# Two attentions mixed by a gate, on one core: other steps for four loads, for a copy of sums, for the output projections and for one score in eight

## The chip, the cores and the metric

The kernel runs on one core of one Trainium2 chip. The metric is the device time of one execution in microseconds (us). The figure for a kernel is the median of its runs. A difference of about 0.3% (3.1 us) is what a measurement of this kernel can tell from no change.

## The reference

Two attention layers over the same input x (2048 tokens, width 448, 16 heads of 28) are mixed by a gate for each token. Layer A is linear attention on learned features, layer B is full softmax attention:

```python
x = A_x
g = _sigmoid((x * gate_w).sum(-1, keepdims=True))
...
phi_q = jnp.concatenate([_softmax(pq, axis=-1), _softmax(-pq, axis=-1)], axis=-1)
...
num = jnp.einsum("bhqf,bhfd->bhqd", phi_q, kv)
...
scores = jnp.einsum("bhqd,bhkd->bhqk", q, k) * scale
p = _softmax(scores, axis=-1)
o = jnp.einsum("bhqk,bhkd->bhqd", p, v)
...
return g * a + (1 - g) * b
```

The data are float32; the projections and the scores run as matmuls of 128x512 in fp32r.

## The kernel before, in words

The first third of the span makes the projections, layer A and the first row maxima for layer B. What the change touches is the rest: layer B's attention, which the loop at L1110 writes out step by step.

**Steps.** The 16 heads are four groups g of four heads, and the queries four blocks qb of 512. One pair (g, qb) is called gq here, 0 to 15. Each gq has 16 steps, one for each 128 keys kt, so there are 256 steps s. In a step, `scores` (L846) makes four score tiles st of 128 keys x 512 queries, one for each head, each in its own PSUM bank, and ScalarE (ACT) takes their exponential into four tiles p (L868). One step later `values` (L982) multiplies p by the values into pv, one bank that gathers the sums of four heads over the 16 steps. So TensorE (PE) does scores of step s, then values of step s-1.

**Visits.** The exponent needs each query's largest score subtracted. These maxima nm are found ahead of the scores that use them, by 180 visits (`mx_visit`, L306). A visit is four small matmuls pm into four banks (L323). ACT reads one bank with a relu (L327, tile rl), VectorE (DVE) reads two with a plain maximum (L334) and one with a maximum of that bank plus the rl of the visit before (L331). One visit in four has three plain maxima instead, and the next has one more to do.

**Single and double steps.** Up to step 104 the loop takes two steps at a time with one visit, in 52 rounds (eight scores, sixteen value matmuls, one visit). From 105 to 232 it takes one step with one visit, in 128 rounds. After 232 there are no visits, and it takes two steps again.

**Banks.** There are eight PSUM banks: one for pv, and seven that `cycle_banks` (L917) deals out. Scores and visits read and write different ones in turn. Three banks (`late3`) come from scores and visits of earlier rounds; four (`visit`) were the banks of the visit just before. In a single step the scores take the three of late3 and the first of visit, which is the one that ACT's relu of that visit reads. After 232 one bank is set aside for the output projections (`spare`), and six go round. The order in which L911 asks for the banks first decides which place in PSUM, and so which earlier reader, each of them follows.

**Loads.** The stacked keys kst (five buffers, four for each group) and queries qst (two buffers, one for each gq) come from DRAM in four DMAs of 224 KB each (`load_k`, `load_q`, `load_stack`), and the maxima go into a row of qst by four DMAs of 2 KB (`load_nm`, L838). All DMAs are issued by SyncE's queue (SP). The order on PE, DVE, ACT and POOL is the order in which the program is written; the order on SP is made by the framework's scheduler from the same program. SP is strictly in order: a DMA that waits for POOL or DVE holds up all behind it. Each DMA also uses one of eight completion semaphores in turn, and waits until that semaphore's last DMA has landed.

**After the last key of a gq**, `finish` (L1026) copies pv out on DVE (f1, L400, tile oUb), which frees the pv bank; a little later it sends the sums' denominators through DRAM (f2: den, rd, and rs, which holds them spread over all rows), multiplies on POOL (f3, L421) and splits the result in two parts on POOL (f4, L429 and L430), which go to DRAM as od (L1046), or for the last group straight to the projections. POOL also subtracts keys from each other for the visits (kc, L197).

**Projections.** In the last group, when a query block is done, `project` (L994) makes an output tile of 128 tokens by eleven matmuls into the spare bank (pob, L110), and DVE adds it to layer A's part (acc, L1000), which frees that bank. `PROJ` names the step of the first of four tiles of a block; before the change they run at the end of the round in which that step lies.

Of the kernel before, what the change touches and what calls it, by code (L numbers as in the profile page):

```python
# [8 lines left out]
F32 = mybir.dt.float32  # L9
F32R = mybir.dt.float32r  # L10
U32 = mybir.dt.uint32
AF = mybir.ActivationFunctionType
# [5 lines left out]
P = 128  # L18
# [5 lines left out]
NG = 4  # L24
NT = S // P
NQ = S // 512
SCALE = DH ** -0.5
# [3 lines left out]
LOWEST = -3.0e38  # L31
LAST = 232
OUTS = (200, 238, 246, 206)
PROJ = (234, 242, 250)


def f32(ap):
# [4 lines left out]
def gated_mix_kernel(ctx, tc, xT, wqkB, wvB, wvA, wkAT, wqAT, phi, woA, woB,  # L42
# [260 lines left out]
    flats += [(gq, kb, qt, h, 64 * gq + 16 * kb + 4 * qt + h) for gq in range(GM + 1, NG * NQ)  # L303
              for qt in range(4) for kb in range(4) for h in range(4)]

    def mx_visit():  # L306


        take_diffs(2)
        f = mxs["f"]  # L310
        todo = flats[f:f + 4]
        fins = mxs["fin"][:1 if todo and todo[0][1] == 0 else None]
        del mxs["fin"][:len(fins)]
        mxs["f"] = f + len(todo)
        if todo:
            gq, kb, qt, _, col = todo[0]
            g, qb = divmod(gq, NQ)
            if kb == 1 and qt in (0, QM) and gq + 1 < NG * NQ and ("qc", gq + 1) not in mxs:
                mx_query(gq + 1)
            pm = mx_banks(f, kb)  # L320
            for j in sorted(range(4), key=lambda j: j != kb):
                js = slice(32 * j, 32 * j + DH)
                nc.tensor.matmul(pm[j], mxs[("qc", gq)][js, qt * P:(qt + 1) * P],  # L323
                                 mxs[("kc", g, kb)][js, :], start=True, stop=True,
                                 tile_position=(32 * j, 0))
            rl = late_p.tile([P, 512], F32, tag="rl", name=f"rl{f}", bufs=3)
            nc.scalar.activation(rl, pm[kb], AF.Relu if kb < 3 else AF.Copy)  # L327
            for j in sorted({0, 1, 2, 3} - {kb}, key=lambda j: j == kb - 1):
                if j == kb - 1:
                    r = mxs["rl"]  # L330
                    nc.vector.tensor_tensor_reduce(r, pm[j], r, 1.0, LOWEST, ALU.add, ALU.max,  # L331
                                                   part[:, col + j:col + j + 1])
                else:
                    nc.vector.tensor_reduce(part[:, col + j:col + j + 1], pm[j], AX.X, ALU.max)  # L334
            mxs["rl"] = rl
            if kb == 3:
                mxs["fin"].append(lambda: nc.vector.tensor_reduce(
                    part[:, col + 3:col + 4], rl, AX.X, ALU.max))
            if qb == NQ - 1 and g + 1 < NG:
                if qt == 2 and kb == 3:  # L340
                    mx_load(g + 1, 0)
                if qt == 3 and kb < 3:
                    mx_load(g + 1, kb + 1)
            if qt == 3 and kb == 3:
                mx_reduce(gq)
        for fn in fins:
            fn()
# [492 lines left out]
    def load_k(g, kb):  # L840
        kst_of[(g, kb)] = load_stack(kst[(4 * g + kb) % 5], k_d[g], kb * 512, (0, 1, 0, 1))
# [1 line left out]
    NS = NG * NQ * NT  # L843
    pv_of, pts, late, mids = {}, {}, {}, {}

    def scores(s, i):  # L846

        gq, kt = divmod(s, NT)
        g, qb = divmod(gq, NQ)

        def score(j, st):
            nc.tensor.matmul(st, kst_of[(g, kt // 4)][:, j, (kt % 4) * P:(kt % 4 + 1) * P],  # L852
                             qst_of[gq][:, j, :], start=True, stop=True)

        if s == 0:
            p = at.tile([P, 2, 512], F32, name=f"p{s}_{i}")
            st = ps_mx(f"st{s}_{i}", i)
            for jl in range(2):
                score(2 * i + jl, st[:, jl, :])
            nc.scalar.activation(p, st, AF.Exp, scale=SCALE)  # L860
            pts.setdefault(s, []).extend([p[:, 0, :], p[:, 1, :]])
            return
        sts = [bank(b, f"st{s}_{j}") for j, b in enumerate(i)]
        for j in range(4):
            score(j, sts[j])
        pts[s] = [late_p.tile([P, 512], F32, tag="p", name=f"p{s}_{j}", bufs=12) for j in range(4)]
        for j in range(4):
            nc.scalar.activation(pts[s][j], sts[j], AF.Exp, scale=SCALE)  # L868

    qst = [stack("qst0", False)]  # L870
    kst = [stack(f"kst{i}", True) for i in range(5)]
# [35 lines left out]
    def bank(i, nm):  # L907
        return ps2.tile([P, 512], F32, tag=f"g{i}", name=nm, bufs=1)


    for i in (2, None, 3, 4, 0, 1, 5, 6):  # L911
        if i is None:
            ps2.tile([P, 512], F32, tag="pv", name="pv_first", bufs=1)
        else:
            bank(i, f"first{i}")

    def cycle_banks(n):  # L917

        x, y = late3[:], visit[:]
        if spare:  # L920
            b = [(free.append(free.pop(0)), free[-1])[1] for _ in range(4 * n)]
        elif n == 1:
            b = x + y[:1]
            late3[:], visit[:] = [b[2], b[3], y[3]], [b[0], y[1], b[1], y[2]]
        else:
            b = x + y[:2] + [x[0], y[2], x[1]]
            late3[:], visit[:] = b[5:], [y[3], b[2], b[3], b[4]]
        return b
# [65 lines left out]
    def project(qb, oT, tl):  # L994

        t = qb * 4 + tl
        acc = acc_of[qb][:, tl, :]
        po = bank(spare[0], f"pob{t}")
        run(po[:, :D], first_passes(qb, tl) + out_passes(oT, tl * P, woB_s, NG - 1))
        nc.vector.scalar_tensor_tensor(acc, po[:, :D], gate1[:, t:t + 1], acc,  # L1000
                                       op0=ALU.mult, op1=ALU.add)
        nc.sync.dma_start(out[0, t * P:(t + 1) * P, :], acc)
# [23 lines left out]
    def finish(gq, s):  # L1026

        st = {}
        g, qb = divmod(gq, NQ)
        last = gq == NG * NQ - 1  # L1030

        def f1():
            st["n"] = normalize1(late_p, [pv_of[gq]], f"b{gq}", 1)

        def f2():
            st["n"] = normalize2(late_p, *st["n"], f"b{gq}", 1, False)

        def f3():
            st["n"] = normalize3(*st["n"], 1)

        def f4():
            st["o"], = normalize4(late_p, st["n"], f"b{gq}", 1)
            if g < NG - 1:
                for j in range(4):
                    r = (4 * g + j) * DH
                    nc.sync.dma_start(o_d[r:r + DH, :, qb * 512:(qb + 1) * 512],  # L1046
                                      f32(st["o"][32 * j:32 * j + DH]))

        if last:
            finish_last(gq)  # L1050
            return
        f1()
        late.setdefault(s + 3, []).append(f2)
        late.setdefault(s + 7, []).append(f3)
        late.setdefault(s + 8, []).append(lambda: acts.append(f4))
        if g == NG - 1:
            for tl in range(4):
                mids[PROJ[qb] + tl] = lambda tl=tl: project(qb, st["o"], tl)

    def finish_last(gq):  # L1060

# [43 lines left out]

    first = 2 * (LAST - len(flats) // 4)
    s = 0
    while s < NS + 16:  # L1110
        n = 2 if 0 < s <= first or LAST < s < NS - 1 else 1
        steps = range(s, s + n)
        s += n
        take_acts()
        for t in steps:
            gq, kt = divmod(t, NT)
            g, qb = divmod(gq, NQ)
            if t >= NS:
                break
            if t in (0, 3):  # L1120
                load_k(0, 2 + t // 3)
            if g + 1 < NG and qb == NQ - 1 and kt % 4 == 2:
                load_k(g + 1, kt // 4)
            if kt == 12 and gq + 1 < NG * NQ:
                load_q(gq + 1)
            if kt == (12 if gq + 1 < 14 else 14) and gq + 1 < NG * NQ - 1:
                load_nm(gq + 1)
            if t in OUTS:
                load_out(OUTS.index(t))
            if g == NG - 1 and kt == (12 if qb < 2 else 14):  # L1130
                load_acc(qb)
        if 0 < steps[0] < NS:
            b = cycle_banks(n)
            for i, t in enumerate(steps):
                scores(t, b[4 * i:4 * i + 4])
        if steps[0] == NS:
            tail_open()
            tail_fill(3)
        for t in steps:
            if 0 < t <= NS:  # L1140
                values(t - 1)
                if t % NT == 0:
                    finish(t // NT - 1, t)
        if steps[0]:
            mx_visit()
        if mxs["f"] == len(flats):
            mx_fin()
        for t in steps:
            if t in mids:
                mids.pop(t)()  # L1150
        if mxs["f"] == len(flats) and not spare:
            spare_open()
        if NG * NQ - 1 in nm_of and NG * NQ - 1 in qst_of:
            load_nm(NG * NQ - 1)
        for t in steps:
            for fn in late.pop(t, []):
                fn()
# [68 lines left out]
```

## Time and profile before

| | |
|---|---|
| median of 3 runs | 1031.74 us (1030.77 to 1033.37) |
| the profiled execution, its own time | 1033.35 us |
| its span, first to last instruction | 1031.6 us |
| granted TensorE clock, mean | 0.995 |
| PE / ACT / DVE / POOL busy | 98% / 80% / 63% / 24% |
| scores and values, busy (L852, L989) | 304.7 and 261.1 us |
| exponentials (L868), 1020 of them | 519.5 us |
| plain maxima (L334), 405 of them | 258.8 us |

A matmul's record begins when it is handed on and ends by a model, so PE seems busy almost always, also where it waits for a moment for a bank; the chain of waits and the weight loads' idle times show such moments. The timeline merges neighbouring instructions of one form into a row, with the count and, in brackets, the idle time before the first and what ended it. A row of the chain of waits has its start, its length and the work. Where an engine waits for several semaphores, the one that came last by the profile is named, and it can be the wrong one.

### The profile page before, as it was taken

Reading aid. Unit: us, or ns where it says so; the run is one execution under the profiler, and the core shown is the slowest. Engines: PE = TensorE matmul, PEld = TensorE weight load, DVE = VectorE, ACT = ScalarE, POOL = GpSimd, SP = SyncE. Lnnn points to the kernel's source line nnn. Section 1 sums busy time; section 2 is a strip of 40 time slices with the busy share of each in tenths; the row PEclk is TensorE's granted clock in tenths of the full one; section 3 lists DMA queues with packets and bytes.
Section 4 is the critical chain, followed back from the end, with each engine's and each line's share of the span. In section 5 each row is a group of like instructions: output and inputs, shape, how many; then the busy total and the mean of one; then the engine's idle time right before and its main releaser. Section 6 shows DMA issues by size and latency. Waiting matters only on the chain.

```text
span 1031.6 us, 17673 instructions
## 1 busy us (share of the span) xinstructions
PE 1014.5 (98%) x6344; PEld 573.2 (56%) x6344; DVE 647.5 (63%) x1335; ACT 824.8 (80%) x1534; POOL 251.1 (24%) x218
## 2 busy tenths in 40 slices
PE   8999999999999999999899999999999999999998
PEld 7877777878777644444344443333333333335666
DVE  5466777898754634454344568788888787884112
ACT  4355555487855699999799999999999999997662
POOL 1225544679635900220110210010110101100010
PEclk9999999999999999999899999999999999999999
DMA  8873010122233851232522323622232445310441
GB/s 293 289 245 112 31 51 31 42 57 79 80 106 94 182 120 37 67 90 74 110 64 63 73 64 84 131 70 58 70 83 56 110 113 155 84 37 29 134 140 57
DMA packets 64570, 99.62 MB, mean 97 GB/s; under 512 B 18134, under 2 KB 24902, under 8 KB 64482
## 3 DMA queue, kind: packets, MB, share of 16 engines
q1 hardware_dynamic: 64482, 98.49, 35.1%
q8 instruction: 50, 0.82, 0.4%
q14 instruction: 38, 0.31, 0.1%
HBM read 70.29 MB, written 27.78 MB: 95 GB/s over the span
## 4 chain that ended last, share of the span: by engine, by line
PE 91%; DVE 3%; DMA 3%; POOL 1%; ACT 1%; SPq 0%; issue 0%; POOLq 0%; DVEq 0%; ACTq 0%
PE st L852 27%; PE pv L989 23%; PE pm L323 7%; PE pqk L110 5%; PE poa L110 4%; PE pk L128 4%; PE pva L128 3%; PE pmb L286 3%; PE pob L110 3%; PE pq L110 2%; PE pvb L110 2%; PE pvb L128 2%; PE pn L534 1%; PE pqk L636 1%; DMA kst<-qkd 1%; PE pft L522 1%
## 5 line engine op out<-in xcount | busy, mean ns | idle before, releaser
L868 ACT ACTIVATE p<-st 128x512 f32<-128x512 f32 x1020 | 519.5, 624 | 35.2 <-PE st L852 35.2
L334 DVE TENSOR_REDUCE part<-pm 128x1 f32<-128x512 f32 x405 | 258.8, 686 | 172.7 <-PE pm L323 168.5
L852 PE MATMUL st<-qst,kst 128*128 128x512 f32 x1024 | 304.7, 428 | 5.6 <-DMA qst<-nm 4.6
L989 PE MATMUL pv<-p,vb 128*32 128x512 f32 x2048 | 261.1, 605 | 0.0
L852 PEld LDWEIGHTS st<-qst,kst 128*128 128x128 f32 x1024 | 175.2, 188 | 120.6 <-issue 48.9
L421 POOL TENSOR_TENSOR oUb<-oUb,rsb 128x512 f32<-128x512 f32 x15 | 19.4, 1291 | 505.6 <-DMA rsb<-rdb 310.8
L291 DVE CUSTOM_DVE_ANT_0 rl<-pmb,rl 128x512 f32<-128x512 f32 x152 | 98.3, 684 | 58.1 <-ACT rl L289 58.0
L323 PEld LDWEIGHTS pm<-kc,qc 28*128 28x128 f32 x720 | 34.8, 182 | 152.0 <-ACT p L868 102.2
L327 ACT ACTIVATE rl<-pm 128x512 f32<-128x512 f32 x180 | 107.6, 598 | 11.6 <-PE pm L323 4.5
L289 ACT ACTIVATE rl<-pmd 128x1024 f32<-128x1024 f32 x76 | 78.1, 1028 | 38.2 <-PE pmd L286 31.0
L989 PEld LDWEIGHTS pv<-p,vb 128*32 128x32 f32 x2048 | 50.7, 109 | 83.4 <-issue 79.0
L331 DVE CUSTOM_DVE_ANT_0 rl<-pm,rl 128x512 f32<-128x512 f32 x135 | 92.0, 681 | 0.0
L323 PE MATMUL pm<-kc,qc 28*128 28x512 f32 x720 | 91.3, 495 | 0.6 <-POOL kc L197 0.6
L110 PE MATMUL pqk<-XH,wB 128*128 128x512 f32 x192 | 61.0, 405 | 1.8 <-DVE ev L574 1.8
L573 ACT CAST ev<-pqk 128x512 fp32r<-128x512 f32 x28 | 16.0, 588 | 39.4 <-PE pqk L110 34.6
L1000 DVE SCALAR_TENSOR_TENSOR acc<-pob,gate,acc 128x448 f32<-128x448 f32 x12 | 8.2, 684 | 59.9 <-PE pob L110 59.9
L110 PE MATMUL poa<-woA_s,oTa 128*128 128x448 f32 x192 | 43.4, 375 | 0.0
L110 PEld LDWEIGHTS pqk<-XH,wB 128*128 128x128 f32 x192 | 36.2, 193 | 11.0 <-DVE ev L574 2.3
L128 PE MATMUL pk<-wkA_s,XH 128*128 128x448 f32 x128 | 39.5, 382 | 0.0
L286 PE MATMUL pmd<-kp,qp 28*128 28x512 f32 x152 | 38.0, 496 | 0.7 <-DVE part L291 0.7
L110 PEld LDWEIGHTS poa<-woA_s,oTa 128*128 128x128 f32 x192 | 34.9, 189 | 6.2 <-issue 3.2
L128 PE MATMUL pva<-wvA_s,XH 128*128 128x450 f32 x128 | 37.9, 372 | 0.0
(155 smaller groups left out, 1197.7 us busy)
## 6 DMA issues: line engine op xcount, KB each, us to landing
qkd<-ev SPq DMA_DIRECT2D x28, 512.0 KB
qst<-qkd SPq DMA_DIRECT2D x64, 224.0 KB
kst<-qkd SPq DMA_DIRECT2D x64, 224.0 KB
od<-oTb SPq DMA_DIRECT2D x48, 112.0 KB
rsa<-rda SPq DMA_DIRECT2D x8, 512.0 KB
rsb<-rdb SPq DMA_DIRECT2D x15, 256.0 KB
gad<-ga SPq DMA_DIRECT2D x16, 224.0 KB
acc<-gad SPq DMA_DIRECT2D x4, 896.0 KB
```

The costliest lines, as they stand in the source:

```text
L110: nc.tensor.matmul(dst, l, r, start=i == 0, stop=i == len(todo) - 1)
L128: nc.tensor.matmul(dst[:, :n], l, r, start=i == 0, stop=i == len(todo) - 1, skip_group_check=True)
L286: nc.tensor.matmul((pb if j < 2 else pd)[:, j % 2, :], qc[js, qt * P:(qt + 1) * P], kc[js, :], start=True, stop=True, tile_position=(32 * ...
L289: nc.scalar.activation(rl, pd, AF.Relu)
L291: nc.vector.tensor_tensor_reduce(rl[:, i, :], pb[:, i, :], rl[:, i, :], 1.0, LOWEST, ALU.add, ALU.max, part[:, col + i:col + i + 1])
L323: nc.tensor.matmul(pm[j], mxs[("qc", gq)][js, qt * P:(qt + 1) * P], mxs[("kc", g, kb)][js, :], start=True, stop=True, tile_position=(32 * ...
L327: nc.scalar.activation(rl, pm[kb], AF.Relu if kb < 3 else AF.Copy)
L331: nc.vector.tensor_tensor_reduce(r, pm[j], r, 1.0, LOWEST, ALU.add, ALU.max, part[:, col + j:col + j + 1])
L334: nc.vector.tensor_reduce(part[:, col + j:col + j + 1], pm[j], AX.X, ALU.max)
L852: nc.tensor.matmul(st, kst_of[(g, kt // 4)][:, j, (kt % 4) * P:(kt % 4 + 1) * P], qst_of[gq][:, j, :], start=True, stop=True)
L868: nc.scalar.activation(pts[s][j], sts[j], AF.Exp, scale=SCALE)
L989: nc.tensor.matmul(pv[32 * j:32 * j + 32, :], vb[kt // 8][:, kt % 8, 4 * g + j, :], pt[j], start=kt == 0, stop=kt == NT - 1, tile_position ...
```

## The change

It has four parts, and a different order of the first requests for banks.

1. **Loads at other steps.** The next group's first two key stacks are loaded at steps 2 and 7 of the last query block, and its other two at steps 0 and 2 of its own first block; before, all four were loaded at 2, 6, 10 and 14 of the last block. The queries of the next gq are loaded at step 5 in place of 12. The maxima stay at step 12 or 14.
2. **Sums copied between a visit's parts.** In the double rounds, f1 stands between the visit's second and third read on DVE; before, it stood ahead of the first. In single steps it stays ahead of the visit.
3. **Projections ahead of four scores each.** PROJ is one step later, and a projection stands ahead of the scores of its own step, not at the end of the round.
4. **Five and three scores.** From step 106 to 231 the even steps make the first score of the odd step after them as well, and the odd steps make the remaining three. The five take all of late3 and the first two visit banks; the three take all of late3 and none of the visit banks. This happens 63 times.

```diff
-PROJ = (234, 242, 250)
+PROJ = (235, 243, 251)
...
+                seen += 1
+                if seen == 2:
+                    mid()
...
-        sts = [bank(b, f"st{s}_{j}") for j, b in enumerate(i)]
-        for j in range(4):
+        sts = {j: bank(b, f"st{s}_{j}") for j, b in zip(js, i)}
+        for j in js:
             score(j, sts[j])
...
-    for i in (2, None, 3, 4, 0, 1, 5, 6):
+    for i in (3, 4, 1, 2, 5, 6, 0, None):
...
+        elif n == 3:
+            b = x
+            late3[:], visit[:] = [x[1], y[3], x[2]], [y[0], y[1], x[0], y[2]]
+        elif n == 5:
+            b = x + y[:2]
+            late3[:], visit[:] = [x[2]] + y[:2], [x[0], y[2], x[1], y[3]]
...
-        f1()
+        copies.append(f1)
...
+    ahead = range(first + 3, LAST, 2)
...
-            if g + 1 < NG and qb == NQ - 1 and kt % 4 == 2:
+            if g + 1 < NG and qb == NQ - 1 and kt in (2, 7):
                 load_k(g + 1, kt // 4)
-            if kt == 12 and gq + 1 < NG * NQ:
+            if g and qb == 0 and kt in (0, 2):
+                load_k(g, 2 + kt // 2)
+            if kt == 5 and gq + 1 < NG * NQ:
                 load_q(gq + 1)
...
-            b = cycle_banks(n)
-            for i, t in enumerate(steps):
-                scores(t, b[4 * i:4 * i + 4])
+            heads = [(t, j) for t in steps for j in range(t in ahead, 4)]
+            heads += [(s, 0)] * (s in ahead)
+            b = cycle_banks(len(heads))
+            for t in dict.fromkeys(t for t, _ in heads):
+                if t in mids:
+                    mids.pop(t)()
+                js = [j for u, j in heads if u == t]
+                scores(t, b, js)
+                b = b[len(js):]
...
+        if n == 1 or mxs["f"] == len(flats):
+            take_copies()
         if steps[0]:
-            mx_visit()
+            mx_visit(take_copies)
```

Three places show what moves. The first is SP's queue ahead of step 64, where the second group of heads begins. kst0, kst1, kst2 and kst4 are buffers of key stacks, qst0 and qst1 the two of queries; kst4 is the new group's first stack, kst0 its second, kst1 its third; rd, rs and od are what `finish` of gq 2 sends, and nm4 the new group's first maxima. Before:

```order
L826 DMA qst0_3650<-qkd_68 28x4x512
L826 DMA kst0_3652<-qkd_68 28x4x512 x2
L414 DMA rdb2_5494<-denb2_5366 128x16
L826 DMA kst0_3652<-qkd_68 28x4x512
L415 DMA rsb2_5495<-rdb2_5494 128x1x512
L826 DMA kst0_3652<-qkd_68 28x4x512
L826 DMA kst1_3655<-qkd_68 28x4x512
L1046 DMA od_73<-oTb2_0_5609 56x1x512 x4
L826 DMA kst1_3655<-qkd_68 28x4x512 x3
L826 DMA qst0_3650<-qkd_68 28x4x512 x3
L838 DMA qst0_3650<-nm4_4327 1x16x32 x4
L826 DMA kst2_3658<-qkd_68 28x4x512 x4
```

And the same place now:

```order
L830 DMA qst0_3650<-qkd_68 28x4x512 x3
L418 DMA rdb2_5494<-denb2_5378 128x16
L830 DMA qst0_3650<-qkd_68 28x4x512
L419 DMA rsb2_5495<-rdb2_5494 128x1x512
L830 DMA kst0_3652<-qkd_68 28x4x512 x4
L1057 DMA od_73<-oTb2_0_5613 56x1x512 x4
L842 DMA qst0_3650<-nm4_4327 1x16x32 x4
L830 DMA kst1_3655<-qkd_68 28x4x512 x4
```

All four DMAs of the queries now stand ahead of od, the third key stack stands behind nm4, and nothing stands between od and nm4.

The second place is PE in two single steps, 120 and 121. st120_0 is the first score of step 120, p119 the exponentials of step 119, pm a visit's matmuls. Before, each step has four scores:

```order
L852 MATMUL st120_0_7549<-qst1_3667,kst1_3655 128x512
L852 MATMUL st120_1_7550<-qst1_3667,kst1_3655 128x512
L852 MATMUL st120_2_7551<-qst1_3667,kst1_3655 128x512
L852 MATMUL st120_3_7552<-qst1_3667,kst1_3655 128x512
L989 MATMUL pv7_7317<-p119_0_7523,vb0_3152 32x512
L989 MATMUL pv7_7317<-p119_1_7524,vb0_3152 32x512
L989 MATMUL pv7_7317<-p119_2_7525,vb0_3152 32x512
L989 MATMUL pv7_7317<-p119_3_7526,vb0_3152 32x512
```

Now the first score of step 121 stands with those of step 120, and three are left for the next round:

```order
L856 MATMUL st120_3_7556<-qst1_3667,kst1_3655 128x512
L856 MATMUL st121_0_7569<-qst1_3667,kst1_3655 128x512
L1000 MATMUL pv7_7317<-p119_0_7500,vb0_3152 32x512
L1000 MATMUL pv7_7317<-p119_1_7529,vb0_3152 32x512
L1000 MATMUL pv7_7317<-p119_2_7531,vb0_3152 32x512
L1000 MATMUL pv7_7317<-p119_3_7533,vb0_3152 32x512
L323 MATMUL pm268_3_7580<-kc2_3_6951,qc8_6178 128x512
L323 MATMUL pm268_0_7577<-kc2_3_6951,qc8_6178 128x512
L323 MATMUL pm268_1_7578<-kc2_3_6951,qc8_6178 128x512
L323 MATMUL pm268_2_7579<-kc2_3_6951,qc8_6178 128x512
L856 MATMUL st121_1_7597<-qst1_3667,kst1_3655 128x512
L856 MATMUL st121_2_7598<-qst1_3667,kst1_3655 128x512
```

The count of scores, values and visits is the same; one score in eight has moved ahead of a block of values and a visit.

The third place is PE behind step 234, with the second and third projection of a block (pob1, pob2). Before, they follow each other:

```order
L989 MATMUL pv14_11349<-p235_3_11682,vb1_3644 32x512
L110 MATMUL pob1_11711<-woB_s_3978,oL0_10430 128x448 x8
L110 MATMUL pob1_11711<-woB_s_3978,oTb12_0_11047 128x448 x3
L110 MATMUL pob2_11725<-woB_s_3978,oL0_10430 128x448 x8
L110 MATMUL pob2_11725<-woB_s_3978,oTb12_0_11047 128x448 x3
L852 MATMUL st237_0_11753<-qst0_3650,kst0_3652 128x512
```

Now four scores stand behind each projection:

```order
L856 MATMUL st235_3_11678<-qst0_3650,kst4_3664 128x512
L110 MATMUL pob1_11691<-woB_s_3978,oL0_10434 128x448 x8
L110 MATMUL pob1_11691<-woB_s_3978,oTb12_0_11055 128x448 x3
L856 MATMUL st236_0_11705<-qst0_3650,kst0_3652 128x512
L856 MATMUL st236_1_11706<-qst0_3650,kst0_3652 128x512
L856 MATMUL st236_2_11707<-qst0_3650,kst0_3652 128x512
L856 MATMUL st236_3_11708<-qst0_3650,kst0_3652 128x512
L1000 MATMUL pv14_11349<-p234_0_11645,vb1_3644 32x512
```

The second projection stands between the two steps' scores, and the third waits until the values of both steps are through.

More of the change, by code (lines that the diff above doesn't have):

```diff
@@ L304, in gated_mix_kernel, with mx_visit @@
               for qt in range(4) for kb in range(4) for h in range(4)]
-    def mx_visit():
+    def mx_visit(mid):
         take_diffs(2)
@@ L327, in mx_visit @@
             nc.scalar.activation(rl, pm[kb], AF.Relu if kb < 3 else AF.Copy)
+            seen = 0
             for j in sorted({0, 1, 2, 3} - {kb}, key=lambda j: j == kb - 1):
@@ L844, in gated_mix_kernel, with scores @@
     pv_of, pts, late, mids = {}, {}, {}, {}
-    def scores(s, i):
+    def scores(s, i, js=range(4)):
         gq, kt = divmod(s, NT)
@@ L862, in scores @@
             return
-        sts = [bank(b, f"st{s}_{j}") for j, b in enumerate(i)]
-        for j in range(4):
+        sts = {j: bank(b, f"st{s}_{j}") for j, b in zip(js, i)}
+        for j in js:
             score(j, sts[j])
-        pts[s] = [late_p.tile([P, 512], F32, tag="p", name=f"p{s}_{j}", bufs=12) for j in range(4)]
-        for j in range(4):
-            nc.scalar.activation(pts[s][j], sts[j], AF.Exp, scale=SCALE)
+        for j in js:
+            p = late_p.tile([P, 512], F32, tag="p", name=f"p{s}_{j}", bufs=12)
+            nc.scalar.activation(p, sts[j], AF.Exp, scale=SCALE)
+            pts.setdefault(s, []).append(p)
     qst = [stack("qst0", False)]
@@ L920, in cycle_banks @@
         if spare:
-            b = [(free.append(free.pop(0)), free[-1])[1] for _ in range(4 * n)]
-        elif n == 1:
+            b = [(free.append(free.pop(0)), free[-1])[1] for _ in range(n)]
+        elif n == 4:
             b = x + y[:1]
             late3[:], visit[:] = [b[2], b[3], y[3]], [b[0], y[1], b[1], y[2]]
+        elif n == 3:
[4 more added lines that the diff above has]
+            late3[:], visit[:] = [x[2]] + y[:2], [x[0], y[2], x[1], y[3]]
         else:
@@ L1058, in finish, with take_copies @@
                 mids[PROJ[qb] + tl] = lambda tl=tl: project(qb, st["o"], tl)
+    copies = []
+    def take_copies():
+        while copies:
+            copies.pop()()
     def finish_last(gq):
@@ L1143, in gated_mix_kernel @@
                     finish(t // NT - 1, t)
+        if n == 1 or mxs["f"] == len(flats):
+            take_copies()
         if steps[0]:
-            mx_visit()
+            mx_visit(take_copies)
         if mxs["f"] == len(flats):
             mx_fin()
-        for t in steps:
-            if t in mids:
-                mids.pop(t)()
         if mxs["f"] == len(flats) and not spare:
```

## The prediction, made before the changed kernel was run

> **What bounds the kernel now.** I read the page first: the engines' shares, the chain that ended last by engine, then the stretches that the change touches.
>
> ```profile
> PE 1014.5 (98%) x6344; PEld 573.2 (56%) x6344; DVE 647.5 (63%) x1335; ACT 824.8 (80%) x1534; POOL 251.1 (24%) x218
> PE 91%; DVE 3%; DMA 3%; POOL 1%; ACT 1%; SPq 0%; issue 0%; POOLq 0%; DVEq 0%; ACTq 0%
> ```
>
> PE carries 91% of the chain, so only what shortens PE's stream or its waits counts. DMA's 3% is about 31 us; two pieces of it, 6.07 and 6.15, are met below. The windows of the single steps show that ACT has almost no room there either:
>
> ```profile
> 676.00:930.00 254.00, 254.00 (x1562) 99.41 (x1561) 205.83 (x415) 248.80 (x488) 22.89 (x21) 1.00 0.34 83
> ```
>
> PE is busy all of the 254 us and ACT 248.8 of them. Next I looked for holes: the timeline ahead of step 64, and the chain behind it.
>
> ```profile
> 481.86 0.36 SPq L414 DMA_DIRECT2D rdb<-denb  x1
> ...
> 483.35 0.57 SPq L415 DMA_DIRECT2D rsb<-rdb  x1
> ...
> 492.93 3.75 SPq L1046 DMA_DIRECT2D od<-oTb  x4
> ...
> 495.11 1.93 PE L989 MATMUL pv<-p,vb 128*32 128x512 f32 x16
> ...
> 498.20 1.27 SPq L826 DMA_DIRECT2D qst<-qkd  x3
> ...
> 499.52 2.47 SPq L838 DMA_DIRECT2D qst<-nm  x4
> 499.55 1.92 PE L989 MATMUL pv<-p,vb 128*32 128x512 f32 x16
> ...
> 507.73 2.05 PE L852 MATMUL st<-qst,kst 128*128 128x512 f32 x4 [4.64 <-DMA qst<-nm]
> ```
>
> ```profile
> 501.47 6.07 DMA qst<-nm
> ...
> 509.78 3.20 PE pv L989 x16
> ...
> 513.41 2.44 PE st L852 x8
> 515.85 1.85 PE pv L989 x16
> ```
>
> A double round is 4.44 us (values at 495.11 and 499.55). The next values come at 509.78, 10.23 later, and those after them 6.07 later. PE idles 4.64 us for the new group's maxima, whose DMA takes 6.07 us to land behind the key and query loads, which od held up on SP.
>
> **The change part by part.** *Loads at step 64.* The excess is 10.23 - 4.44 + 6.07 - 4.44 = 7.4 us, of which 0.27 belongs to the copy (below): 7.1. The idle time is 4.64; the rest is a slower clock, which the windows show:
>
> ```profile
> 505.60:512.40 6.80, 4.67 (x20) 1.76 (x20) 0.00 (x0) 2.07 (x4) 0.00 (x0) 0.50 0.64 126
> ```
>
> Half clock for 6.8 us, of which PE worked 4.67: about 2.3 lost. The Trainium skill (TensorE: Matmul & The Clock Gate, Terms) puts the penalty at the throttled time times one minus the clock's share, 3.4 us here; the trace disagrees, since part of that time PE was idle anyway. By the page this term would be 8.0 and the sum 15.5.
>
> In the new order nothing stands between od and nm on SP. od still starts at 492.93, since POOL's chain behind rs sets that, and is issued by 496.7; nm takes 2.47 more, so its last DMA goes out at about 498.6. A small DMA with nothing ahead lands in under 1.5 us (rd at 481.86, and rs, which needs it, at 483.35); with the bulk ahead it took 6.07. So the maxima are there between 500.1 and 504.7. The first score of step 64 is wanted at about 502.9 (499.55 + 1.85 for values, 0.43 for the visit, 1.1 for four scores). The wait left is 0 to 1.8; the small DMA is the nearer row, so 0, and 0.1 for the waits themselves: **7.0 us** gained (5.3 to 7.1). Third and fourth key stack now follow nm and are first read 8 and 12 steps later, four double rounds or 17.8 us and more; the queries moved ahead of od wait on SP only for buffers read out long ago.
>
> *Steps 107 and 128.* Two smaller holes:
>
> ```profile
> 600.04 6.15 DMA rsb<-rdb
> ...
> 609.82 1.28 POOL kc L197
> ...
> 611.14 0.82 PE pm L323 x4
> ```
>
> ```profile
> 656.91 2.55 SPq L838 DMA_DIRECT2D qst<-nm  x4
> ```
>
> ```profile
> 664.75 0.76 PEld L852 LDWEIGHTS st<-qst,kst 128*128 128x128 f32 x4 [0.98 <-ACT rl L327]
> ```
>
> At 128 the maxima are issued at 656.91 behind the queries; the weight load idles 0.98 where 0.24 is usual. The relu that is named frees a bank for the fourth score only; the first needs the maxima. Queries and keys now stand ahead of od there: **0.7** (0 to 0.75). At 611 the visit waits for POOL's key difference, which stands behind f3 and f4, and those wait for rs; PE loses 0.6 idle and some 0.4 in the longer pm row, 1.0. Before, rs was issued behind a block of key loads that waited for PE; now it stands ahead of them, and is held only by rd's landing, about 1 to 2 us earlier: **0.9** (0 to 1.0).
>
> *The copy.* In the double rounds f1 goes first and the plain maxima wait for it:
>
> ```profile
> 398.40 0.69 DVE L400 COPY oUb<-pv 128x512 f32<-128x512 f32 x1 [2.27 <-PE pv L989]
> ...
> 399.01 1.28 DVE L334 TENSOR_REDUCE part<-pm 128x1 f32<-128x512 f32 x2
> ```
>
> ```profile
> 470.52 2.44 PE st L852 x8
> ...
> 475.24 2.17 PE st L852 x8
> ```
>
> Eight scores take 2.44 behind a copy and 2.17 in the next round: 0.27, six times, 1.6. Now the copy follows the maxima and frees pv later. The maxima then start at about 398.8 and end at 400.06, the copy at 400.75; the values want pv 0.43 + 2.17 after the visit at 398.2, so at 400.8. It just fits: **1.5** (0 to 1.6). Denominators leave 1.6 us later, covered by f2's three steps.
>
> *Projections.*
>
> ```profile
> PE pob L110 <- DVE acc L1000: 2.3, 3, 0.8
> ```
>
> Three times a projection follows another and waits for DVE's sum. Four scores (about 1.0 us, half of a block of 1.96 to 2.17) now cover DVE's 0.7. Projections and scores are the same in number: **2.2** (2.0 to 2.3).
>
> *First requests for banks.* The same view has one row for step 1:
>
> ```profile
> PE st L852 <- ACT p L860: 0.3, 1, 0.3
> ```
>
> The first scores took banks that step 0's second exponential read. They now take others: **0.3** (0 to 0.3).
>
> *Five and three scores.* A single step in the timeline, and two of a step's scores by themselves:
>
> ```profile
> 802.55 0.51 PE L323 MATMUL pm<-kc,qc 28*128 28x512 f32 x4
> 802.99 1.25 PE L852 MATMUL st<-qst,kst 128*128 128x512 f32 x4
> 803.09 0.60 ACT L327 ACTIVATE rl<-pm 128x512 f32<-128x512 f32 x1
> ...
> 803.58 2.06 ACT L868 ACTIVATE p<-st 128x512 f32<-128x512 f32 x4
> 803.74 0.19 PEld L852 LDWEIGHTS st<-qst,kst 128*128 128x128 f32 x1 [0.22 <-ACT rl L327]
> 804.17 1.06 PE L989 MATMUL pv<-p,vb 128*32 128x512 f32 x8
> ...
> 805.16 0.51 PE L323 MATMUL pm<-kc,qc 28*128 28x512 f32 x4
> ```
>
> ```profile
> 842.46 0.40 PE L852 MATMUL st<-qst,kst 128*128 128x512 f32 x1
> ```
>
> ```profile
> 842.93 0.45 PE L852 MATMUL st<-qst,kst 128*128 128x512 f32 x1
> ```
>
> The step is 805.16 - 802.55 = 2.61. It is a ring: visit, relu, the relu's bank, fourth score, values, visit. The fourth score's weights go in at 803.74, 0.05 behind the relu's end, and its matmul lasts 0.45 where the second's lasts 0.40: 0.05 lost in each step. With five and three, the three need no visit bank; the five still meet the relu at their fourth. One hold of two goes: 63 x 0.05 = 3.2 at best. Against it: the third of the three scores needs the bank of the fifth, so its exponential. From the visit's start the relu begins at +0.54, the first exponential 0.49 later, the others (2.06 - 0.63) / 3 = 0.48 apart; the fifth ends at 0.54 + 0.49 + 4 x 0.48 + 0.63 = +3.58. Its bank is wanted at 2.61 + 0.25 (the extra score) + 0.44 + 0.34 = +3.64. A margin of 0.06: each 0.1 beyond it costs 6.3. I take **2.0** (-6 to 3.2).
>
> *Sum:* 7.0 + 0.7 + 0.9 + 1.5 + 2.2 + 0.3 + 2.0 = 14.6. The profiled execution took 1033.35 with a span of 1031.6; it would be 1018.75. The median of the runs shown is 1031.74, 1.6 below it, so I predict 1031.74 - 14.6 = **1017.1**.
>
> **The rivals.**
>
> 1. *Five and three bring nothing.* The kernel is then at 1019.1. For it: 0.05 is a difference of two modelled records, and the fifth score waits for DVE where the fourth waited for ACT. Against it: the weight load idles for the relu 0.22 us each time. The Trainium skill (TensorE: Matmul & The Clock Gate, Step-by-step) says that PE's queue pulls weight loads ahead of running matmuls; by that rule the late bank would cost the array nothing. The row of 803.74 shows one that wasn't pulled ahead. Chance 0.20.
> 2. *The fifth exponential is late.* Each 0.1 per pair beyond the margin costs 6.3 in place of the gain of 2.0: 1025.4. For it: ACT is busy 248.8 of 254. Against it: the sum above, and the relu of the five's visit delays nobody. Chance 0.12. The same mechanism makes the kernel **slower**: the other parts bring 12.6, so it decides from (12.6 + 3.1) / 63 = 0.25 a pair; at 0.3 the time is 1038.0. It needs exponentials 0.08 longer each than their row. Chance 0.03; a further 0.03 near 0.2 a pair, no change.
> 3. *The maxima still land late at 64.* At the far end 1.8 stays: 1018.9, and if od itself comes later by a little, 1020. Chance 0.10.
> 4. *The loads don't move in effect*, since SP waits for POOL and DVE as before: without the first three terms, 8.6 less, 1025.7. The order speaks against it: the bulk has passed od. Chance 0.05.
>
> **How the numbers follow.** My forecast has 0.47, and its time is the sum's. All terms at their best give 16.3, 1015.4, and the runs shown scatter by 1 to either side. The range **1013.5 to 1024.0** holds the forecast and rivals 1 and 3, and about half of rival 2. Faster by over 0.3% (below 1028.6): 0.94; within it 0.03; slower 0.03.
>
> **What would show it.** In the profile after: no idle time for nm ahead of step 64, and a clock of 1.0 there; rounds of eight scores at 2.17 behind a copy; no row of pob waiting for acc; pairs of single steps at about 5.19 in place of 5.22, with only the fourth of the five behind the relu. A weight load of the third of three scores that idles for an exponential would prove rival 2. Values that wait for the copy would take my 1.5 away. A wait for nm or kst at 64, 72, 128 or 136 would prove the loads wrong.

## The result, and the profile after

| | before | after |
|---|---|---|
| median of the runs compared, us | 1032.11 (4 runs, 1030.77 to 1033.37) | 1016.29 (4 runs, 1015.14 to 1016.56) |
| ratio of the times | | 0.9845, 95% interval 0.9828 to 0.9862 |
| span of the profiled execution, us | 1031.6 | 1014.8 |
| granted TensorE clock, mean | 0.995 | 1.0 |

The kernel is 1.55% faster: 15.8 us by the medians, 16.8 by the two profiled spans. The prediction was 1017.1. After the change the code lines are a little further down: scores are L856, exponentials L872, values L1000, sums L1011, the maxima's DMAs L842.

The page after: engines and the chain that ended last by engine.

```profile
PE 1004.8 (99%) x6344; PEld 566.7 (56%) x6344; DVE 647.5 (64%) x1335; ACT 818.1 (81%) x1534; POOL 250.9 (25%) x218
PE 95%; DVE 3%; ACT 1%; DMA 1%; issue 0%; POOL 0%; DVEq 0%; ACTq 0%; POOLq 0%
```

PE's share of the chain rises from 91 to 95%, DMA's falls from 3 to 1%. PE's busy time falls too, by 9.7, with the same 6344 instructions: a matmul's record starts when it is handed on, so a matmul that waits for its bank, or runs at half clock, was counted as busy.

Step 64, from the timeline of SP and then of PE, and the window over both (length, PE, PEld, DVE, ACT and POOL busy, clock, DMA share, GB/s):

```profile
493.21 3.45 SPq L1057 DMA_DIRECT2D od<-oTb  x4
496.70 2.48 SPq L842 DMA_DIRECT2D qst<-nm  x4
499.29 1.81 SPq L830 DMA_DIRECT2D kst<-qkd  x4
```

```profile
500.72 2.33 PE L856 MATMUL st<-qst,kst 128*128 128x512 f32 x8
```

```profile
500.00:507.00 7.00, 7.00 (x43) 3.34 (x40) 3.50 (x7) 6.98 (x15) 0.00 (x0) 1.00 0.65 135
```

od starts at the old time, the maxima follow it at once, and the eight scores of steps 63 and 64 stand in one row with no idle time. The clock stays at 1.00.

Steps 107 and 128: SP's two small DMAs and POOL's key difference with the visit that needs it, then the maxima of step 128 and the weight load of its scores.

```profile
587.71 0.36 SPq L418 DMA_DIRECT2D rdb<-denb  x1
...
589.29 0.56 SPq L419 DMA_DIRECT2D rsb<-rdb  x1
```

```profile
599.54 1.27 POOL L197 TENSOR_TENSOR kc<-kc,kd 28x512 fp32r<-28x512 f32 x1
601.54 0.51 PE L323 MATMUL pm<-kc,qc 28*128 28x512 f32 x4
```

```profile
643.51 3.12 SPq L842 DMA_DIRECT2D qst<-nm  x4
```

```profile
661.67 0.30 PEld L856 LDWEIGHTS st<-qst,kst 128*128 128x128 f32 x2 [0.25 <-ACT p L872]
```

The same pair in the trace of before:

```profile
596.40 0.35 SPq L414 DMA_DIRECT2D rdb<-denb  x1
```

There rs followed at 600.04, 3.64 later; now it goes out 1.58 behind rd, and POOL is done at 600.81, 0.73 ahead of the visit. The maxima of step 128 leave 18 us ahead of their use.

A round behind a copy, from the timeline and, for the scores, from the chain:

```profile
398.35 1.29 DVE L335 TENSOR_REDUCE part<-pm 128x1 f32<-128x512 f32 x2 [2.67 <-PE pm L323]
399.56 0.68 DVE L404 COPY oUb<-pv 128x512 f32<-128x512 f32 x1
400.38 1.92 PE L1000 MATMUL pv<-p,vb 128*32 128x512 f32 x16
```

```profile
398.29 2.15 PE st L856 x8
```

The scores take 2.15 and not 2.44. The copy ends at 400.24, 0.14 ahead of the values that need its bank.

A block of projections in the chain, then the timeline of single steps with the weight loads of five and of three scores:

```profile
929.23 2.43 PE pob L110 x11
931.65 0.93 PE st L856 x4
932.59 2.35 PE pob L110 x11
```

```profile
800.74 0.51 PE L323 MATMUL pm<-kc,qc 28*128 28x512 f32 x4
...
803.06 0.51 PE L323 MATMUL pm<-kc,qc 28*128 28x512 f32 x4
803.50 1.47 PE L856 MATMUL st<-qst,kst 128*128 128x512 f32 x5
...
805.90 0.51 PE L323 MATMUL pm<-kc,qc 28*128 28x512 f32 x4
```

```profile
804.24 0.32 PEld L856 LDWEIGHTS st<-qst,kst 128*128 128x128 f32 x2 [0.21 <-ACT rl L327]
...
806.33 0.54 PEld L856 LDWEIGHTS st<-qst,kst 128*128 128x128 f32 x3 [0.25 <-ACT p L872]
```

The step of three takes 2.32 (800.74 to 803.06), that of five 2.84, together 5.16 where two steps took 5.22. The fourth of the five still waits for the relu; the three go through in one row. The views of waits count it: before, then after.

```profile
PEld st L852 <- ACT rl L327: 39.8, 179, 1.0
```

```profile
PEld st L856 <- ACT rl L327: 25.2, 117, 0.2
```

62 waits fewer, one for each pair but one. Of the projections' waits for DVE's sum, PE's own row of 2.3 us is gone; a row of weight loads stays (total, times, longest), with at most 0.3 us each, hardly more than the 0.25 that a weight load idles in the rows above without holding anything up:

```profile
PEld pob L110 <- DVE acc L1011: 1.7, 6, 0.3
```

**Where the 16.8 went**, from the starts of each step's first score in the two traces:

| stretch | before | after | less | forecast |
|---|---|---|---|---|
| round of step 63 and 64 | 11.51 | 4.55 | 6.96 | 7.0 |
| hole at 107 | 1.01 | 0 | 1.01 | 0.9 |
| hole at 127 and 128 | 0.69 | 0 | 0.69 | 0.7 |
| six rounds behind a copy | 28.27 | 26.75 | 1.5 | 1.5 |
| steps 233 to 253, with three blocks of projections | 68.30 | 65.14 | 3.16 | 2.2 |
| steps 0 to 2 | 7.24 | 6.95 | 0.29 | 0.3 |
| 63 pairs of single steps | 5.218 each | 5.168 each | 3.1 | 2.0 |
| sum | | | 16.7 | 14.6 |

Ahead of the first score the two traces differ by 0.16. That stretch has the same code in every kernel here, but takes from 358.5 to 361.2 in different executions. The experiments are therefore read by stretches behind the first score. Where only one time is given for an experiment, it is that of a single run.

### The profile page after: what moved, and what is told of

It reads as the page before. It is cut to its first block, busy times and chain, and to the rows that moved or that the text cites. A ratio compares the mean times of both kernels' runs of the same rounds, so it can differ in the third digit from the quotient of the medians.

```text
span 1014.8 us, 17693 instructions
## 1 busy us (share of the span) xinstructions
PE 1004.8 (99%) x6344; PEld 566.7 (56%) x6344; DVE 647.5 (64%) x1335; ACT 818.1 (81%) x1534; POOL 250.9 (25%) x218
## 4 chain that ended last, share of the span: by engine, by line
PE 95%; DVE 3%; ACT 1%; DMA 1%; issue 0%; POOL 0%; DVEq 0%; ACTq 0%; POOLq 0%
PE st L856 28%; PE pv L1000 24%; PE pm L323 8%; PE pqk L110 5%; PE poa L110 4%; PE pk L128 4%; PE pva L128 4%; PE pmb L286 3%; PE pob L110 3%; PE pq L110 2%; PE pvb L110 2%; PE pvb L128 2%; PE pn L538 1%; PE pqk L640 1%; PE pft L526 1%; DVE featq L453 1%
## 5 line engine op out<-in xcount | busy, mean ns | idle before, releaser
L872 ACT ACTIVATE p<-st 128x512 f32<-128x512 f32 x1020 | 525.1, 639 | 26.4 <-PE st L856 26.4
L856 PE MATMUL st<-qst,kst 128*128 128x512 f32 x1024 | 299.5, 422 | 0.1
L1000 PE MATMUL pv<-p,vb 128*32 128x512 f32 x2048 | 259.7, 601 | 0.0
L856 PEld LDWEIGHTS st<-qst,kst 128*128 128x128 f32 x1024 | 171.0, 187 | 101.6 <-ACT p L872 39.3
L327 ACT ACTIVATE rl<-pm 128x512 f32<-128x512 f32 x180 | 111.5, 620 | 10.4 <-PE pm L323 10.0
L1000 PEld LDWEIGHTS pv<-p,vb 128*32 128x32 f32 x2048 | 50.5, 108 | 96.0 <-issue 93.6
L1011 DVE SCALAR_TENSOR_TENSOR acc<-pob,gate,acc 128x448 f32<-128x448 f32 x12 | 8.2, 684 | 50.8 <-PE pob L110 50.8
```

Source lines behind the costliest of these rows:

```text
L872: nc.scalar.activation(p, sts[j], AF.Exp, scale=SCALE)
L1000: nc.tensor.matmul(pv[32 * j:32 * j + 32, :], vb[kt // 8][:, kt % 8, 4 * g + j, :], pt[j], start=kt == 0, stop=kt == NT - 1, tile_position ...
```

## The experiments

### The loads alone

The kernel before with the first part of the change (steps of `load_k` and `load_q` as in the diff above), nothing else.

> The kernel before with the first part of the change alone (key stacks at steps 2 and 7 and at 0 and 2 of the own first block, queries at step 5). My theory, by the sum on record: step 64 gives 7.0, step 107 0.9 and step 128 0.7, so 8.6 less than before, about 1023.3 by the median; the round that begins at step 63 falls from 11.5 to some 4.6 us with no idle time for the maxima. Rival 3 (maxima still late): that round stays above 5.5 and the time above 1025. Rival 4 (loads don't move in effect): the round stays at 11.5 and the time at 1031.7.

Measured: 1023.65 (1022.9 to 1024.6) against 1032.76 for the kernel before, ratio 0.9912 (0.9898 to 0.9927). From the timeline, steps 63 and 64:

```profile
500.08 2.34 PE L852 MATMUL st<-qst,kst 128*128 128x512 f32 x8
```

The round takes 4.56 and both holes are gone: 6.95 + 1.01 + 0.70 = 8.7 by stretches, 9.1 by the medians. Rivals 3 and 4 fall.

### Five and three scores alone

The kernel before with the fourth part (`ahead`, `heads` and the two new branches of `cycle_banks`).

> The kernel before with five and three scores alone. My theory: one hold of the fourth score's weight load behind the relu in each pair goes, as in the kernel after, where pairs take 5.167 in place of 5.220: 63 x 0.053 = 3.3 less, about 1028.6. Rival 1 (weight loads are pulled ahead, so the late bank costs the array nothing, and the gain of the pairs came from another part of the change): pairs stay at 5.22 and the time within 0.5 of before.

Measured: 1030.53 (ten runs, 1028.66 to 1037.84), ratio 0.9986 (0.9968 to 1.0003). The whole time can't tell it from no change; the pairs can: 5.166, as in the kernel after. A part of what it gained elsewhere it gave back at the holes that the loads still made here:

```profile
613.10 0.82 PE L323 MATMUL pm<-kc,qc 28*128 28x512 f32 x4 [0.70 <-POOL kc L197]
```

```profile
666.74 1.40 PE L856 MATMUL st<-qst,kst 128*128 128x512 f32 x5 [1.17 <-DMA kst<-qkd]
```

Steps 105 to 108 take 8.84 (before 8.83), and 122 to 130 take 21.82 (before 21.57), where four pairs should have gained 0.2: PE comes sooner to POOL and to the maxima, which come when they did. (The row at 666.74 names a DMA of keys. Step 128 reads its group's first key stack, which was loaded long before, so the maxima are what it waits for.) About 0.5 of 3.1 goes so. The round at 63 took 12.50 here; it took 12.52 in the third experiment, whose code is the old one there, so this 1.0 is scatter from execution to execution and no work of the five and three.

### The fourth score in a bank that VectorE reads

The kernel before, with a later reader ahead of the fourth score:

```diff
-            b = x + y[:1]
-            late3[:], visit[:] = [b[2], b[3], y[3]], [b[0], y[1], b[1], y[2]]
+            b = x + y[1:2]
+            late3[:], visit[:] = [b[2], b[3], y[3]], [b[0], y[0], b[1], y[2]]
```

> The kernel before, where in single steps the fourth score takes the bank that DVE's first plain maximum reads, in place of the one that ACT's relu reads. By the ring theory of the prediction (visit, reader of the bank, fourth score, values, visit) the step follows that reader: the first maximum ends about 0.12 later than the relu after the visit's start, so a step takes about 2.73 in place of 2.61, and 128 steps make the kernel about 15 us slower, some 1047. If the ring doesn't bind (PE's stream alone sets the step, as rival 1 has it), the step stays at 2.61 and the time within 1 of before.

Measured: 1050.38. From the timeline of PE, then of the weight loads:

```profile
803.72 0.50 PE L323 MATMUL pm<-kc,qc 28*128 28x512 f32 x4
...
806.46 0.50 PE L323 MATMUL pm<-kc,qc 28*128 28x512 f32 x4
```

```profile
805.04 0.19 PEld L852 LDWEIGHTS st<-qst,kst 128*128 128x128 f32 x1 [0.35 <-DVE part L334]
```

The step is 806.46 - 803.72 = 2.74, 0.13 more, and the load idles for DVE 0.35 in place of 0.22: the same 0.13. So the reader of the fourth score's bank sets the length of a step. 128 x 0.13 = 16.6; in the traces steps 105 to 232 take 17.1 more than before, and the whole kernel is 17.6 above the median of before. The Trainium skill (TensorE: Matmul & The Clock Gate, Step-by-step) has weight loads pulled ahead of running matmuls, where the row groups don't conflict or the load goes to the background weight buffer. In this trace the load of the fourth score, whose bank still has a reader, starts only behind that reader, as its row shows.

### The bank of the fifth score wanted earlier

The kernel after, with the first of the three scores in the fifth's bank:

```diff
-            late3[:], visit[:] = [x[2]] + y[:2], [x[0], y[2], x[1], y[3]]
+            late3[:], visit[:] = [y[1], x[2], y[0]], [x[0], y[2], x[1], y[3]]
```

> The kernel after, where the first of the three scores, not the third, takes the bank of the fifth score. It is then wanted two scores (0.47) earlier. By the working of rival 2 the fifth exponential ends at +3.58 after the visit of the five and the bank was wanted at +3.64, now at about +3.2, so each pair loses 0.3 to 0.4: pairs of 5.5 in place of 5.17 and a time of 1035 to 1041. If exponentials are earlier than that working says, or a late bank is hidden by the weight load, pairs stay at 5.17 and the time within 1 of the kernel after.

Measured: 1037.57, pairs of 5.52. From one timeline, the five's visit and exponentials, then the three's first weight load:

```profile
804.84 0.51 PE L323 MATMUL pm<-kc,qc 28*128 28x512 f32 x4
...
805.87 2.55 ACT L872 ACTIVATE p<-st 128x512 f32<-128x512 f32 x5
...
808.47 0.53 PEld L856 LDWEIGHTS st<-qst,kst 128*128 128x128 f32 x3 [0.59 <-ACT p L872]
```

The fifth exponential ends at 808.42, +3.58 after the visit, as the prediction had it, and the load follows 0.05 later. It idles 0.59 in place of 0.25. A pair loses 0.35 where the bank was wanted 0.47 earlier, so the kernel after has 0.12 to spare; the prediction had 0.06. Rival 2's mechanism is real, and the kernel after stays 0.12 short of it.

### Queries or keys back

The kernel after with `load_q` at step 12 again:

```diff
-            if kt == 5 and gq + 1 < NG * NQ:
+            if kt == 12 and gq + 1 < NG * NQ:
```

> The kernel after with the queries loaded at step 12 again; two of their four DMAs (448 KB) then stand between od and the maxima on SP at step 64, where before there were six of keys and queries. My theory is that the wait at 64 goes by the bulk ahead of the maxima: two cost 0.85 of issue and about a third of the 6.07 that six made, so the maxima land at about 502, ahead of the 502.9 at which they are wanted: the round at 63 stays at 4.55 to 4.7 and the time within 1 of the kernel after. Rival (any bulk ahead of the maxima, or SP's wait for od alone, makes them late): 3 us or more of wait there, and half clock behind it.

And with the four key stacks together again:

```diff
-            if g + 1 < NG and qb == NQ - 1 and kt in (2, 7):
+            if g + 1 < NG and qb == NQ - 1 and kt % 4 == 2:
                 load_k(g + 1, kt // 4)
-            if g and qb == 0 and kt in (0, 2):
-                load_k(g, 2 + kt // 2)
```

> The kernel after with all four key stacks of the next group in its last query block again; one stack, four DMAs (896 KB), then stands between od and the maxima at step 64. By the bulk theory they are issued 1.7 later than in the kernel after and land some 4 us after that, at about 504.3: the round at 63 grows from 4.55 to about 6 (5 to 7.5, with a slower clock if PE idles long enough), and step 128 loses up to 0.75, since there also keys stand ahead of the maxima. Rival (only the queries' move matters, since keys and maxima go to different tiles): 4.55 there.

Measured: 1017.50 with the queries back and 1021.02 with the keys back. Steps 63 and 64 with the queries back:

```profile
500.73 2.46 PE L856 MATMUL st<-qst,kst 128*128 128x512 f32 x8
```

The keys' case: SP, then PE, then two windows, at the wait and behind it:

```profile
495.44 1.82 SPq L830 DMA_DIRECT2D kst<-qkd  x4
497.31 2.48 SPq L842 DMA_DIRECT2D qst<-nm  x4
```

```profile
499.66 1.24 PE L856 MATMUL st<-qst,kst 128*128 128x512 f32 x4
504.36 1.17 PE L856 MATMUL st<-qst,kst 128*128 128x512 f32 x4 [3.45 <-DMA kst<-qkd]
```

```profile
500.00:504.00 4.00, 0.90 (x4) 0.37 (x2) 1.69 (x4) 2.31 (x5) 0.00 (x0) 1.00 0.96 181
```

```profile
504.30:509.00 4.70, 4.64 (x24) 1.36 (x24) 0.00 (x0) 2.07 (x4) 0.00 (x0) 0.64 0.47 94
```

| DMAs of 224 KB between od and the maxima | round of step 63 |
|---|---|
| none (after) | 4.55 |
| 2 (queries back) | 4.68 |
| 4 (keys back) | 9.73 |
| 6 (before) | 11.51 |

The row at 504.36 names a DMA of keys: by its time the one issued at 499.89, behind the maxima. Those are keys of the fourth stack, and step 64 reads the first, loaded long before, so it is the maxima that it waits for. They are issued by 499.8 in both kernels; two DMAs ahead of them cost 0.13 and four 5.18. The DMAs move 181 GB/s there, an estimated 1.27 us for each. Two more make 2.5, and with the keys back PE is at these scores 1.1 sooner (499.66 against 500.73), so 0.13 + 2.5 + 1.1 = 3.7 is the idle time that this sum gives, worked out behind the run, and 3.45 is measured. The round expected at about 6 (5 to 7.5) was a miss. The landing expected at 504.3 fits; what was wrong is when the maxima are wanted: 502.9 came from the trace of before, and here PE has the four scores of step 63 done at 500.9. The rest of the 5.18 is half clock: 4.7 us at 0.64 with PE busy throughout lose 4.7 x 0.36 = 1.7.

The queries' case has the hole at 107 back, 0.89 of it, which its expectation didn't name:

```profile
602.22 0.83 PE L323 MATMUL pm<-kc,qc 28*128 28x512 f32 x4 [0.49 <-POOL kc L197]
```

```profile
587.80 0.36 SPq L418 DMA_DIRECT2D rdb<-denb  x1
590.02 1.16 SPq L177 DMA_DIRECT2D kc<-qkd  x3
591.29 0.57 SPq L419 DMA_DIRECT2D rsb<-rdb  x1
```

rs stands behind three loads of visit keys (L177) that wait for PE, as before the change, and leaves 3.49 behind rd. So the queries' move made step 107. At step 64 the two parts overlap: with the queries at their old place the keys' move takes the round from 11.51 to 4.68, 6.83 of the 6.96; with the keys at theirs the queries' move takes it from 11.51 to 9.73, 1.78. The keys' move is nearly enough there, and the queries' move is not. Neither brings the hole at 128 back (expected up to 0.75 with the keys: a miss): either move is enough for it.

### The copy first again

```diff
-        copies.append(f1)
+        f1()
```

> The kernel after with the copy ahead of the visit's parts again in double rounds. My theory: the six rounds behind a copy grow from 4.46 to 4.72 and the kernel by 1.5. Rival (the copy's cost went because the loads moved, or the values now wait for it): rounds as in the kernel after, no change.

Measured: 1017.94. In the chain the scores behind a copy are as in the kernel before:

```profile
470.00 2.43 PE st L856 x8
```

Rounds behind a copy take 4.64 and five times 4.71 to 4.72, 1.5 more in all, less 0.1 that the round at step 31 wins. The copy's term stands by itself.

### The projections at the rounds' ends again

```diff
-PROJ = (235, 243, 251)
+PROJ = (234, 242, 250)
...
-                if t in mids:
-                    mids.pop(t)()
...
+        for t in steps:
+            if t in mids:
+                mids.pop(t)()
```

> The kernel after with the projections at the end of rounds again. If the move brought the whole 3.2 by which the three blocks of steps 235, 243 and 251 are shorter than before: blocks of 26.3 in place of 25.3, 3.2 more in all, with the wait of pob for acc back at 0.76 each (2.3 of it). Rival (only the 2.2 of the prediction belongs to it, and the rest to the other order of banks or the steps before): blocks grow by 0.75 and the time by 2.2.

Measured: 1019.00. The chain of one block:

```profile
928.09 2.45 PE pob L110 x11
...
934.35 2.46 PE pob L110 x11
...
936.84 0.70 DVE acc L1011
...
937.58 2.50 PE pob L110 x11
```

Steps 235 to 241 take 19.70 in place of 18.70, and the others alike: 1.00, 1.05 and 1.02. The wait is 0.76 each (the third projection starts at 937.58, and the second ends at 936.81); the rest is in the projections' own rows, 2.45, 2.46 and 2.50 here, where those behind four scores take 2.35. Another 0.5 at step 241 goes with this row of the waits (total, times, longest), the first projection of the next block, which comes a step earlier than in the kernel after and has to wait for its input from DRAM (the kernel before has no such wait at that step; why it comes here is not shown):

```profile
PEld pob L110 <- DMA oL<-od: 0.7, 2, 0.5
```

### Four and four scores again

The kernel after with `ahead = range(0)`.

> The kernel after without five and three scores: every single step makes its own four. With the loads' holes gone, the 63 pairs should cost what they do in the kernel before: 5.22 in place of 5.167, 3.3 more by the trace, about 1019.6 by the median. Rival (part of the pairs' gain needs the other edits, or is given back elsewhere, as the time of the kernel with this part alone suggests with its 1.4 to 2.2): 1.4 to 2.2 more, 1017.7 to 1018.5, and pairs between 5.19 and 5.20.

Measured: 1019.29 (1018.38 to 1020.64), ratio to the kernel before 0.9869 (0.9852 to 0.9887). Pairs take 5.222, and steps 105 to 232 take 331.5 in place of 328.1: 3.4. With the loads' holes gone the whole gain of five and three is there. Of what the kernel that has them alone lacks by its trace, about 0.5 is the holes' doing and 1.0 the longer round at 63.

### The first banks again

The kernel after with the old order of requests.

```diff
-    for i in (3, 4, 1, 2, 5, 6, 0, None):
+    for i in (2, None, 3, 4, 0, 1, 5, 6):
```

> The kernel after with the old order of first requests for banks. My theory: steps 0 to 2 take 7.24 again in place of 6.96, 0.3 more, and nothing else moves. Rival (the order also decides which bank follows which reader later, in rounds or in the tail): some other stretch moves by more than 0.2.

Measured: 1015.24, below the median of the kernel after. Steps 0 to 2 take 7.24 as expected and no other stretch moves by more than 0.1, but behind the first score the two executions take 654.7 and 654.8. A term of 0.3 shows in its stretch and not in the time.

## Why the prediction was right, and where its sizes were off

- *Loads at step 64* (7.0): right in mechanism and size, 6.96. The range's lower end, maxima that still wait 1.8, didn't come: they were issued by 499.18 and used from about 501.9 with no wait. The prediction put both moves behind it; by the runs the keys' move alone brings 6.83 of it. In other executions of the old order this round took 12.5, so the term is 7 to 8. One sum beside it is off: 8.0 in place of 7.0 would make 15.6 and not 15.5.
- *Steps 107 and 128* (0.9 and 0.7): 1.01 and 0.69, and rs leaves 2.06 sooner behind rd, the far end of the 1 to 2 of the working. The load behind which rs had stood is that of the visit keys.
- *The copy* (1.5): 1.5. The values find the bank free by 0.14, so "it just fits" held, and the scores behind a copy take 2.15 where 2.17 was the sign to look for.
- *Projections* (2.2): 3.2. The step that failed is the price: three idle times of 0.76 were taken for all of it, with the words that projections and scores are the same in number. They are, but not in time: a projection behind four scores takes 2.35, behind values or behind the wait 2.43 to 2.50. A block has 1.0 to gain, of which the idle row shows three quarters.
- *Five and three* (2.0, with 3.2 at best): 3.1 against the kernel before and 3.4 against four and four. The mechanism was right, and the best case was the case: the margin at the fifth exponential was 0.12 and not 0.06, so nothing was lost there. Taking 2.0 was caution, and the bank moved by two scores shows what it was about: 0.35 a pair, some 21 us in all.
- *Rivals.* 1 falls by the pairs (5.168, against 5.222 without the part) and by the step of 2.74 with a later reader. 2 didn't occur, though it is 0.12 away: the three's first weight load idles 0.25, as much as one that nothing holds (0.24). 3 and 4 fall by the loads alone.
- *The sum* was 14.6; the stretches give 16.7, the medians 15.8. So the sum was short by 2.1 in the traces and by 1.2 in the medians, most of it projections and five and three (1.0 and 1.1). That the time came within 0.8 is in part luck: the sum was taken from a median of 1031.74, and with one more run that median is 1032.11.

## What to carry to other kernels

What a small DMA cost here was decided by the bulk ahead of it in its queue, and only from the point on where the data were wanted (two DMAs of 224 KB cost 0.13, four 5.18): count the bytes between its issue and its use, and move those that nobody needs yet behind it. The price of a wait in a stream of matmuls is the difference from start to start of the same stretch with and without it; the idle row gave three quarters of it for the projections. A part that makes an engine faster brings its whole gain only once that engine no longer waits for others behind it (here 0.5 of 3.1 went into such waits), so the holes go first.

## What the runs showed of the hardware

- Half clock followed the idle time of 3.45 us with the keys back and that of 4.64 before the change, and went on while PE worked again: with the keys back for 4.7 x 0.36 / 0.5 = 3.4 us. After an idle time of 1.17 (a weight load idle 1.45) in the kernel with five and three alone, the clock stayed at full speed, as the window there shows:

```profile
664.00:668.00 4.00, 2.83 (x18) 1.21 (x17) 3.10 (x8) 2.79 (x6) 0.00 (x0) 1.00 0.68 174
```

  The length of the idle time alone does not decide it. In the lead-in, PE idles 1.84 us up to 23.07 in the kernel before, and half clock follows; it idles 3.25 us up to 23.55 in the kernel with the queries back, and none does. The same window in both:

```profile
24.00:28.00 4.00, 4.00 (x13) 3.13 (x12) 0.60 (x2) 0.58 (x1) 0.00 (x0) 0.57 0.80 235
```

```profile
24.00:28.00 4.00, 4.00 (x20) 3.27 (x19) 1.38 (x2) 0.64 (x2) 0.00 (x0) 1.00 0.82 242
```

  What does decide it these runs do not show.

  The Trainium skill (TensorE: Matmul & The Clock Gate, Terms) prices half clock at the throttled time times one minus the share of the clock. With the keys back, where PE works all of that time, this gives the 1.7 measured. At step 64 before the change, where PE idled for part of it, it gave 3.4 against about 2.3.
- A weight load whose bank still has a reader holds PE's stream for the time by which the reader is late, 0.05 for the relu, 0.13 more for the first maximum, though its idle time reads 0.21 to 0.35.
